# When an output block is stored, and which bank one head's product uses: attention and a gated feed-forward on one core

## The chip, the cores and the metric

The kernel runs on one core of a Trainium2 chip. The time is device microseconds for one execution. Engines are named as in the profile: PE (matrix products), PEld (its weight loads), DVE, ACT, POOL, and the queues SP, ACTq and POOLq that issue transfers. A line number such as L828 is a line of the kernel before.

## The reference

The inputs are q, k, v of shape (8, 8, 576, 64): 8 batches, 8 heads, 576 positions, 64 features. The attention is causal by blocks of 64 positions; its output is laid out as 4608 tokens of 512 features and goes through a gated feed-forward. All in float32:

```python
scores = scale * np.matmul(q, k.transpose(0, 1, 3, 2))
scores = np.where(block_i >= block_j, scores, -1e9)      # blocks of 64
attn = softmax(scores)
x = np.matmul(attn, v).transpose(0, 2, 1, 3).reshape(4608, 512)
gate = np.maximum(x @ w_gate, 0.0)                        # 512 -> 1536
val = x @ w_val
out = (gate * val) @ w_out                                # 1536 -> 512
```

## The kernel before

**Two streams of work, one order written by hand.** The attention of batch b runs beside the feed-forward of an earlier tile. A generator, `ffn_gen`, yields after nearly every feed-forward product; a table `AT` gives each step of the attention a place counted in such yields, and the loop at the end (L1515) runs the feed-forward up to that place and then the step. So every engine's instructions stand in the order in which Python writes them.

**The attention.** A round r = 4 b + hp is one pair of heads. Its visit (`s` in the table) makes the scores: the third part goes to a bank of "one" and a bank of "ffn", the first and second to two tiles of "sc". ACT makes exponentials of the third and the first at once, and of the second at the step `e`. DVE or POOL zeroes corners (`c`), steps `a` and `b` multiply the two heads with v (L586, L600), in a bank that the table `HOW` names, and DVE normalises (L523, L525, L532). A transfer transposes the result into xT.

**The matrix product's banks.** There are three pools of accumulators in PSUM: "sc" has two tiles of two banks each, "one" one bank, "ffn" three banks. A tile of a pool takes a buffer that is free again; its first writer waits for the last reader of the tenant before.

**The feed-forward.** Tiles 0 to 7 are the first 512 tokens of each batch, tile 8 (j = B) is the 64 last tokens of all eight. For f from 0 to 11 it makes gate and value, four products each (L858), ACT applies relu to the gate (L868), and DVE multiplies with the value (L878, "hidden f"); both accumulators are "ffn" banks. From f = 4 on, DVE also makes sums and differences of hidden blocks (L743). Gate 10 below is the gate of f = 10.

**The output of tiles 2 to 8.** Token rows and output columns are halved, and seven products of quarter matrices replace eight (`seven_products`). Four output blocks come of it, each 128 x 512 in an "ob" buffer, of which there are four: g (upper left), c12, c22 and c21. In order: ACT copies y into g (L815), DVE adds z (L816) and subtracts m1 (L819); ACT copies y again into c12 (L822); POOL makes c22 = g + c12 (L825); ACT copies z into c21 (L828); POOL adds c21 to g (L830); DVE adds m6 to c22 (L833) and subtracts m7 from g (L838). In tile 8 the last product and subtraction are split in halves (L842, L847).

**The stores.** `store_later` keeps one store in hand: it issues the one in hand and keeps the new one. A store of tiles 2 to 7 is one transfer of 256 KB on ACT's queue (L664). A store of tile 8 is two transfers, one on ACT's queue and one on SP's (L672). The last block of a tile, g, is therefore in hand until the c12 of the next tile is copied, and that of tile 8 until the end of the program (L1521).

Of the kernel before, what the change touches and what calls it, by code (L numbers as in the profile page):

```python
# [17 lines left out]
def kernel(  # L18
# [10 lines left out]
    nc = tc.nc  # L29

    B, H, S, D = q.shape
# [8 lines left out]
    SEVEN = 2  # L40
# [600 lines left out]
    store, late = [], []  # L641
# [16 lines left out]
    def put_block(j, hi, n0, ob, p0, p1):  # L658

        n = slice(n0, n0 + 256)  # L660
        rows = ob.rearrange("q (p n) -> q p n", n=256)
        if j < B:
            r0 = S * j + 256 * hi + 128 * p0
            nc.scalar.dma_start(  # L664
                out[r0 : r0 + 128 * (p1 - p0), n].rearrange("(p q) n -> q p n", q=128),
                rows,
            )
        else:
            by_batch = out.rearrange("(b s) n -> b s n", b=B)
            for i in range(2):  # L670
                b0 = 4 * hi + 2 * p0 + i
                (nc.scalar, nc.sync)[i].dma_start(  # L672
                    by_batch[b0 : b0 + 2 * (p1 - p0) - 1 : 2, 512:576, n].rearrange(
                        "b s n -> s b n"
                    ),
                    rows[64 * i : 64 * i + 64],
                )
# [84 lines left out]
    def seven_products(j, quads, sums):  # L762

        def times(to, which, p, c, first):
            two = wo[c // 2][:, 2 * (c % 2) : 2 * (c % 2) + 2, :]
            t = sevens[c // 2][:, 768 * (c % 2) : 768 * (c % 2) + 768]
            right = {
                5: two[:, 1, 256:512],
                2: two[:, 0, 0:256],
                1: t[:, 0:256],
                3: two[:, 0, 256:512],
                4: two[:, 1, 0:256],  # L780
                6: t[:, 256:512],
                7: t[:, 512:768],
            }[which]
            nc.tensor.matmul(  # L784
                to,
                sums.of(c)[which][:, 128 * p : 128 * p + 128],
                right,
                start=first,
                stop=(c == 5),
                skip_group_check=True,  # L790
            )

        def half(to, p):
            return to[:, 256 * p : 256 * p + 256]

        def whole(to, which, new=True, cs=range(6)):
            for p in range(2):
                for c in cs:
                    times(half(to, p), which, p, c, new and (p, c) == (0, 0))
                    if c % 2:  # L800
                        yield

        def store_later(hi, n0, ob, p0=0, p1=2):
            if store:
                store.pop()()
            store.append(lambda: put_block(j, hi, n0, ob, p0, p1))

        y = psum_ffn.tile([128, 512], FP, name="ffnp")
        z = psum_one.tile([128, 512], FP, name="one")
        for to, which in ((y, 5), (z, 2)):  # L810
            yield from whole(to, which, cs=range(4))
        for to, which in ((y, 5), (z, 2)):
            yield from whole(to, which, new=False, cs=(4, 5))
        g = sb.tile([128, 512], FP, name="ob", bufs=4)
        nc.scalar.copy(g, y)  # L815
        nc.vector.tensor_tensor(out=g, in0=z, in1=g, op=AX.add)  # L816
        m1 = psum_ffn.tile([128, 512], FP, name="ffnp")
        yield from whole(m1, 1)
        nc.vector.tensor_tensor(out=g, in0=m1, in1=g, op=AX.subtract)  # L819
        yield from whole(y, 3, new=False)  # L820
        c12 = sb.tile([128, 512], FP, name="ob", bufs=4)
        nc.scalar.copy(c12, y)  # L822
        store_later(0, 256, c12)
        c22 = sb.tile([128, 512], FP, name="ob", bufs=4)
        nc.gpsimd.tensor_tensor(out=c22, in0=g, in1=c12, op=AX.add)  # L825
        yield from whole(z, 4, new=False)
        c21 = sb.tile([128, 512], FP, name="ob", bufs=4)
        nc.scalar.copy(c21, z)  # L828
        store_later(1, 0, c21)
        nc.gpsimd.tensor_tensor(out=g, in0=g, in1=c21, op=AX.add)  # L830
        m6 = psum_ffn.tile([128, 512], FP, name="ffnp")
        yield from whole(m6, 6)
        nc.vector.tensor_tensor(out=c22, in0=m6, in1=c22, op=AX.add)  # L833
        store_later(1, 256, c22)
        if j < B:
            m7 = psum_ffn.tile([128, 512], FP, name="ffnp")
            yield from whole(m7, 7)
            nc.vector.tensor_tensor(out=g, in0=g, in1=m7, op=AX.subtract)  # L838
            store_later(0, 0, g)
        else:  # L840
            for p in range(2):
                m7 = psum_ffn.tile([128, 512], FP, name="ffnp")[:, 0:256]  # L842
                for c in range(6):
                    times(m7, 7, p, c, c == 0)
                    if c % 2:
                        yield
                nc.vector.tensor_tensor(  # L847
                    out=half(g, p), in0=half(g, p), in1=m7, op=AX.subtract
                )
                store_later(0, 0, half(g, p), p, p + 1)  # L850

    def ffn_gen():
        for j in range(B + 1):
# [3 lines left out]
            def product(to, t, c, f):  # L857
                nc.tensor.matmul(  # L858
                    to,
                    (wg, wv)[t][f // 4][:, c, 128 * (f % 4) : 128 * (f % 4) + 128],  # L860
                    x[:, c],
                    start=(c == 0),
                    stop=(c == 3),
                )

            def relu(gate):
                gate_sb = sb.tile([128, 512], BF, name="gate_sb", bufs=3)
                nc.scalar.activation(gate_sb, gate, AF.Relu)  # L868
                return gate_sb
# [3 lines left out]
            def hidden(gate_sb, val):  # L873
                if len(hT) % 4 == 0:
                    quads.append(sb.tile([128, 4, 512], BF, name="hT", bufs=3))
                h = quads[-1][:, len(hT) % 4, :]
                products.append(
                    nc.vector.tensor_tensor(out=h, in0=gate_sb, in1=val, op=AX.mult)  # L878
                )
                hT.append(h)  # L880
# [52 lines left out]
            for f in range(first, 12):  # L933
                gate = (
                    psum_one.tile([128, 512], FP, name="one")
                    if (j, f) == (1, 2)
                    else psum_ffn.tile([128, 512], FP, name="ffnp")
                )
                val = psum_ffn.tile([128, 512], FP, name="ffnp")
                for t, c in [(t, c) for t in range(2) for c in range(4)]:  # L940
                    product((gate, val)[t], t, c, f)
                    if (t, c) == (0, 3):
                        gate_sb = relu(gate)
                        if sums and f >= 4:
                            sums.step(f)
                    if (t, c) == (1, 3):
                        hidden(gate_sb, val)
                    yield
# [38 lines left out]
    def outs(j):  # L987
        full = [(s, 0, 512) for s in range(4)]
        return full if j < B else full[:3] + [(3, 0, 352), (3, 352, 512)]

    gen = ffn_gen()

    def ffn(n):
        for _ in range(n):
            if next(gen, 0) == 0:
                return
# [11 lines left out]
    dve, act, pool = nc.vector.tensor_copy, nc.scalar.copy, nc.gpsimd.tensor_copy  # L1008
# [7 lines left out]
    with tc.manual_schedule(engines={E.PE, E.DVE, E.Activation, E.Pool, E.SP}):  # L1016
# [82 lines left out]
        def mains_1(hp):  # L1099
# [259 lines left out]
            "r10": ("dve", "one", "ffn", None),  # L1359
            "r11": ("dve", "one", "ffn", None),  # L1360
            "r12": ("dve", "ffn", "sc", None),
            "r13": ("dve", "sc", "ffn", None),
            "r14": ("dve", "ffn", "ffn", None),
            "r15": ("pool", "sc", "sc", None),
            "cv21/1": "dve",
# [152 lines left out]
            place[0] = max(place[0], at)  # L1518
            acts[n]()
        ffn(10**6)  # L1520
        store.pop()()  # L1521
# [1 line left out]
_INS = ['q', 'k', 'v', 'moe_w_gate', 'moe_w_val', 'moe_w_out']  # L1523
_OUTS = [((4608, 512), 'float32')]
# [25 lines left out]
```

## Time and profile before

| | |
|---|---|
| median of 3 runs | 359.91 us (359.58 to 361.34) |
| the profiled execution's own time | 359.73 us |
| its span, first to last instruction | 357.9 us |
| granted PE clock, mean | 0.997 |
| PE, DVE, ACT, POOL busy | 342.8, 207.5, 180.1, 141.2 us |
| tile 2: products of f = 11 end, products with w_out begin | 132.2 us |
| last tile: products with w_out | 342.6 to 351.8 us |
| last tile: the two halves of g on DVE | 353.51 to 354.26 us |

The span runs from the first to the last instruction on the core; the execution's own time has about 1.8 us more around it. Busy time is the sum of an engine's instructions. The list of waits names, for an engine and line, the work whose end released it, with the total, the number of times and the longest. The chain is followed back from the last instruction: at each step to what released it. In the timeline a line is a run of like instructions: start, time, engine, line, what it writes and reads, and in brackets the idle time before it with its releaser.

### The profile page before, as it was taken

How to read it: one execution, taken by the hardware profiler on the slowest of the kernel's cores; microseconds unless marked ns; L12 is line 12 of the kernel's file. 1: busy time of each engine (PE TensorE's matmuls, PEld its weight loads, DVE VectorE, ACT ScalarE, POOL GpSimd, SP SyncE). 2: the span in 40 equal slices, each digit the busy share in tenths (PEclk: the TensorE clock that was granted, in tenths of full speed). 3: DMA queues.
4: the chain of work that ended last, by engine and by line, in shares of the span. 5: the costliest groups of instructions: out<-in, count | busy, mean ns of one | idle time of the engine just before them, and what ended most of it. 6: DMA issues, size and time to landing. Idle time of an engine off the chain costs nothing.

```text
span 357.9 us, 8015 instructions
## 1 busy us (share of the span) xinstructions
PE 342.8 (96%) x3131; PEld 202.0 (56%) x3173; DVE 207.5 (58%) x522; ACT 180.1 (50%) x286; POOL 141.2 (39%) x183
## 2 busy tenths in 40 slices
PE   6899999999999989999999999999999999999993
PEld 2544455545544558555955585557655774484472
DVE  4663445678456584467557663777266735635651
ACT  5932766686345841666256635554555523313320
POOL 4647646597848602590159103930200020020002
PEclk9999999999999999999999999999999999999998
DMA  8999999999999994899369934997400040011005
GB/s 247 296 355 373 320 222 286 194 134 174 173 226 98 148 132 125 95 145 162 82 113 146 159 76 122 135 155 97 139 16 16 16 141 0 2 60 59 1 6 143
DMA packets 155494, 50.02 MB, mean 140 GB/s; under 512 B 134464, under 2 KB 151872, under 8 KB 155456
## 3 DMA queue, kind: packets, MB, share of 16 engines
q0 software_dynamic: 70480, 8.85, 47.7%
q1 hardware_dynamic: 76432, 31.47, 42.8%
q10 hardware_dynamic: 8544, 9.18, 8.0%
q8 instruction: 25, 0.41, 0.5%
q14 instruction: 13, 0.11, 0.1%
HBM read 37.75 MB, written 9.44 MB: 132 GB/s over the span
## 4 chain that ended last, share of the span: by engine, by line
PE 87%; DMA 5%; ACT 3%; POOL 1%; DVE 1%; issue 1%; POOLq 0%; SPq 0%; DVEq 0%; ACTq 0%
PE ffnp L858 49%; PE ffnp L784 12%; PE ffnp L951 5%; PE one L784 5%; PE sc L451 3%; PE one L451 2%; PE ffnp L586 2%; DMA stage<-in_moe_w_gate_dram 2%; PE one L586 1%; DMA stage<-in_k_dram 1%; PE one L858 1%; PE sc L586 1%; PE ffnp L548 1%; ACT attnT L456 1%; DMA out_dram<-ob 1%
## 5 line engine op out<-in xcount | busy, mean ns | idle before, releaser
L878 DVE TENSOR_TENSOR hT<-gate_sb,ffnp 128x512 bf16<-128x512 bf16 x106 | 72.6, 685 | 70.0 <-PE ffnp L858 43.3
L858 PE MATMUL ffnp<-xT,wv 128*128 128x512 bf16 x357 | 99.5, 379 | 1.5 <-issue 0.6
L868 ACT ACTIVATE gate_sb<-ffnp 128x512 bf16<-128x512 f32 x103 | 62.3, 606 | 75.1 <-PE ffnp L858 75.1
L858 PE MATMUL ffnp<-xT,wg 128*128 128x512 bf16 x347 | 96.6, 379 | 1.4 <-DVE xT L630 0.3
L858 PEld LDWEIGHTS <-wv 128*128 128x128 bf16 x432 | 40.0, 98 | 45.1 <-issue 2.9
L825 POOL TENSOR_TENSOR ob<-ob 128x512 f32<-128x512 f32 x7 | 8.8, 1262 | 142.7 <-ACT ob L822 142.7
L858 PEld LDWEIGHTS <-wg 128*128 128x128 bf16 x432 | 39.8, 98 | 43.0 <-issue 3.3
L456 ACT ACTIVATE attnT<-sc 128x1024 bf16<-128x1024 f32 x56 | 57.4, 1042 | 0.0
L784 PEld LDWEIGHTS <-stage 128*128 128x128 bf16 x420 | 40.4, 98 | 6.0
L743 DVE TENSOR_TENSOR stage<-hT 128x512 bf16<-128x512 bf16 (+2 forms) x84 | 38.5, 485 | 0.9
L586 PEld LDWEIGHTS <-attnT 128*128 128x128 bf16 x640 | 26.5, 98 | 12.7 <-DVE attnT L1011 1.6
L784 PE MATMUL ffnp<-stage 128*128 128x256 bf16 x252 | 31.4, 273 | 0.0
L463 ACT ACTIVATE attnT<-one 128x512 bf16<-128x512 f32 (+1 forms) x28 | 15.0, 536 | 23.4 <-PE ffnp L451 23.3
L339 POOL DMA_DIRECT2D v_bf<-in_v_dram x30 | 24.2, 880 | 2.8 <-PE ffnp L858 1.8
L339 POOL DMA_DIRECT2D q_bf<-in_q_dram x20 | 18.2, 924 | 18.1 <-DVE hT L878 13.9
L951 PE MATMUL ffnp<-wo,hT 128*128 128x512 bf16 x90 | 22.8, 379 | 0.3
L451 PEld LDWEIGHTS <-kTm 64*128 64x128 bf16 x384 | 13.1, 94 | 15.6 <-issue 7.9
L451 PE MATMUL sc<-qTm,kTm 64*128 64x512 bf16 (+1 forms) x168 | 17.9, 305 | 1.0 <-DVE xtail L532 1.0
L339 POOL DMA_DIRECT2D k_bf<-in_k_dram x20 | 17.7, 933 | 0.0
L784 PEld LDWEIGHTS <-hT 128*128 128x128 bf16 x168 | 16.4, 98 | 1.9
L833 DVE TENSOR_TENSOR ob<-ffnp,ob 128x512 f32<-128x512 f32 x7 | 4.8, 692 | 21.6 <-POOL ob L825 15.0
L822 ACT COPY ob<-ffnp 128x512 f32<-128x512 f32 x7 | 4.1, 585 | 21.9 <-PE ffnp L784 21.9
(143 smaller groups left out, 459.4 us busy)
## 6 DMA issues: line engine op xcount, KB each, us to landing
out_dram<-ob ACTq DMA_DIRECT2D x32, 256.0 KB, 2.5
stage<-in_moe_w_val_dram SPq DMA_DIRECT2D x6, 512.0 KB, 8.2
stage<-in_moe_w_gate_dram SPq DMA_DIRECT2D x6, 512.0 KB, 8.6
stage<-in_moe_w_out_dram SPq DMA_DIRECT2D x6, 512.0 KB, 10.6
q_bf<-in_q_dram POOLq DMA_DIRECT2D x20, 128.0 KB, 4.5
k_bf<-in_k_dram POOLq DMA_DIRECT2D x20, 128.0 KB, 5.4
v_bf<-in_v_dram POOLq DMA_DIRECT2D x20, 128.0 KB, 6.5
stage<-in_v_dram SPq DMA_DIRECT2D x19, 128.0 KB, 5.6
```

The source lines that it names most:

```text
L339: ins = nc.gpsimd.dma_start(dst, part_of)
L451: nc.tensor.matmul(o, kTm[b % 2][head_of(hh), c, hp, :], qT, start=True, stop=True)
L456: return lambda: nc.scalar.activation(at[:, :, lo : lo + 512], sc, AF.Exp, scale=scale)
L463: nc.scalar.activation(at[:, hh, 1024 : 1024 + w], third[hh][:, 0:w], AF.Exp, scale=scale)
L586: nc.tensor.matmul(av[:, p, :], at[:, col : col + 128], v_bf[b % 2][:, c, h, :], start=(p == 0), stop=(c == p), skip_group_check=True,)
L743: nc.vector.tensor_tensor(out=out.rearrange("p (c n) -> p c n", c=m), in0=a, in1=b, op=op)
L784: nc.tensor.matmul(to, sums.of(c)[which][:, 128 * p : 128 * p + 128], right, start=first, stop=(c == 5), skip_group_check=True,)
L825: nc.gpsimd.tensor_tensor(out=c22, in0=g, in1=c12, op=AX.add)
L858: nc.tensor.matmul(to, (wg, wv)[t][f // 4][:, c, 128 * (f % 4) : 128 * (f % 4) + 128], x[:, c], start=(c == 0), stop=(c == 3),)
L868: nc.scalar.activation(gate_sb, gate, AF.Relu)
L878: nc.vector.tensor_tensor(out=h, in0=gate_sb, in1=val, op=AX.mult)
L951: nc.tensor.matmul(op, hT[f][:, 128 * s : 128 * (s + 1)], wo[f // 4][:, f % 4, n0:n1], start=(f == 0), stop=(f == 11),)
```

## The change

Three things. In tiles 3 to 8 the store in hand is issued behind the relu of the second gate (f = 1), so the block g of the tile before leaves there and not behind the next c12. In tile 8 nothing is kept in hand: each block's two transfers are issued where the block is made, those of c12 both on SP's queue, those of c21 both on ACT's, those of c22 and of the halves of g one on each. And the first head of round 13 (batch 3, the second pair) accumulates its product with v in an "ffn" bank instead of an "sc" tile.

```diff
@@ put_block, tile 8
-                (nc.scalar, nc.sync)[i].dma_start(
+                eng = {(0, 256): nc.sync, (1, 0): nc.scalar}.get((hi, n0))
+                (eng or (nc.scalar, nc.sync)[i]).dma_start(
@@ store_later in seven_products
             if store:
                 store.pop()()
-            store.append(lambda: put_block(j, hi, n0, ob, p0, p1))
+            if j < B:
+                store.append(lambda: put_block(j, hi, n0, ob, p0, p1))
+            else:
+                put_block(j, hi, n0, ob, p0, p1)
@@ ffn_gen, behind relu(gate)
                         if sums and f >= 4:
                             sums.step(f)
+                        if j > SEVEN and f == 1:
+                            store.pop()()
@@ HOW: corners, first head, second head, transpose
-            "r13": ("dve", "sc", "ffn", None),
+            "r13": ("dve", "ffn", "ffn", None),
@@ the end of the program
         ffn(10**6)
-        store.pop()()
+        assert not store
```

## The prediction

> **What bounds the kernel now.** I read the page first: which engine fills the span.
>
> ```profile
> span 357.9 us, 8015 instructions
> ...
> PE 342.8 (96%) x3131; PEld 202.0 (56%) x3173; DVE 207.5 (58%) x522; ACT 180.1 (50%) x286; POOL 141.2 (39%) x183
> ...
> PE 87%; DMA 5%; ACT 3%; POOL 1%; DVE 1%; issue 1%; POOLq 0%; SPq 0%; DVEq 0%; ACTq 0%
> ```
>
> PE is busy for all but 15 us, so only what makes PE wait, or what lies before its start and behind its last product, can move the time. The list of waits shows where the changed lines wait (total, times, longest, in us):
>
> ```profile
> ACT ob L828 <- DMA out_dram<-ob: 12.2, 6, 3.0
> ```
>
> The third output copy of a tile (L828, block c21) waits for a store in six of seven tiles, about 2 us each. Whether that matters differs by place. The stretches 160 to 320 show PE idle for only 0.43, 0.37, 0.53 and 0.10 us, and PE's own list of waits names none there. In the inner tiles the wait is hidden under products. At the end nothing hides it; the chain of its last microseconds:
>
> ```profile
> 347.95 0.02 ACT ob L822
> 347.96 3.44 DMA out_dram<-ob
> 351.42 0.04 ACTq L828
> 351.46 0.04 issue
> 351.50 0.59 ACT ob L828
> 352.09 0.03 POOLq L830
> 352.12 0.07 issue
> 352.19 1.30 POOLq L1545
> 353.49 0.02 issue
> 353.51 0.42 DVE ob L847
> ```
>
> Copy c21 stands behind the store of the tile before (3.44 us), and POOL's sum and DVE's subtractions behind the copy. The timeline gives what else is ready:
>
> ```profile
> 347.70 1.47 PE L784 MATMUL one<-wo,hT 128*128 128x256 bf16 x12
> ...
> 349.01 2.78 PE L784 MATMUL ffnp<-stage 128*128 128x256 bf16 x24
> 350.58 0.69 DVE L833 TENSOR_TENSOR ob<-ffnp,ob 128x512 f32<-128x512 f32 x1 [3.29 <-PE ffnp L784]
> ...
> 351.52 3.85 ACTq L672 DMA_DIRECT2D out_dram<-ob  x5
> ```
>
> Last, tile 2, for the bank edit: one visit's scores stand behind a13's normalisation.
>
> ```profile
> 127.40 0.39 PE L451 MATMUL sc<-qTm,kTm 64*128 64x384 bf16 x4 [0.99 <-DVE xtail L532]
> ...
> 128.15 0.60 ACT L868 ACTIVATE gate_sb<-ffnp 128x512 bf16<-128x512 f32 x1
> ...
> 129.08 0.69 DVE L878 TENSOR_TENSOR hT<-gate_sb,ffnp 128x512 bf16<-128x512 bf16 x1 [1.14 <-PE ffnp L858]
> ...
> 129.82 0.46 PE L586 MATMUL ffnp<-v_bf,attnT 128*128 128x65 bf16 x10
> ```
>
> **The change part by part.** All sums are against the profiled execution: 359.73 us, span 357.9, 1.8 around it; it lies 0.18 under the median 359.91.
>
> *The end of the last tile.* With tile 7's block g stored long before, an ob buffer is free and c21 waits only for its products: they end at 347.70 + 1.47 = 349.17; the c12 copy started 0.09 behind its own, so c21 runs 349.26 to 349.84 (0.585). POOL's c22 sum (1.26 from 348.61) frees POOL at 349.87, so its g sum starts 0.13 behind c21 (before: 352.09 to 352.22) at 349.98 and ends at 351.24. DVE's c22 (350.58 + 0.69) ends at 351.27. Its first half of g needs that, POOL, and six of the twelve m7 products, done at about 351.23: it runs 351.28 to 351.70. The second half needs PE's last product (351.79) and runs 351.89 to 352.30. Before it ended at 353.51 + 0.75 = 354.26: 1.96 earlier.
> The stores: each issue holds its queue (L672: ACT median 0.73, SP 0.60, the 64 KB ones 0.50 to 0.80). Before, ACT issued five from 351.52, the last starting at 354.57. After, c12's two go to SP at 348.56, c21's two to ACT: 349.88 to 351.35; c22's 0.74 to 352.10; g's first half 0.52, from 352.13; the last starts at 352.68. SP's last can start at about 352.5. So 354.57 - 352.68 = 1.89 is gained, the queue giving up 0.07 of the data's 1.96. Ten stores go before and after, and the same barriers follow. Bounds: a landing takes 2.1 to 3.1 in the L672 rows, and 2.4 for the last, so -2.2 to -1.2. I take -1.89, as like stores stand at the end of both.
> The Trainium skill, page "DMA: Bandwidth & Descriptors", section "Issuing engines are not separate DMA queues", says that stores from several engines share the same DMA engines, so a second queue saves only issue time, usually small beside the transfer. It speaks against the re-routing of c12 and c21; the rows here (0.73 of issue to 2.7 of landing) make issue a quarter. By that rule only the data's 1.96 would count, and the total would be 358.40 for 358.47.
>
> *The store at the second gate.* Six stores (g of tiles 2 to 7, 256 KB, L664) leave the place behind the c12 copy and go on ACT's queue behind the second relu of the next tile. Their data: DVE ended tile 3's g at 181.20, and tile 4's second relu starts at 184.16, so nothing waits for DVE; at the last tile it is 323.04 against 324.53. The issue (0.38, at most 0.46) runs while the relu (0.66) does, as it did beside the copy (318.06 and 318.08). Queued behind it is the third relu, which waits for PE anyway: 0.37 idle in tiles 3 to 6, 1.13 in the last two. Cost 0, covered by those waits; bounds 0 and 6 x 0.46 = 2.8 if the cover is gone. On the DMA engines it meets POOL's loads of the next q (from 184.15, landing median 4.5, so in by about 192); SP transposes them at 197.40, so 5 us of slack cover a 2.5 us store: 0. What it leaves: in tiles 3 to 7 c21 comes about 1.2 earlier (tile 3: its products end at 175.75 + 1.47, the copy started at 178.50) and DVE's g 0.7 earlier (m7 ends at 177.06 + 2.78, L838 started at 180.51). PE's idle from 160 to 320 (1.4 in all) bounds a gain; since PE names no wait there, I take 0. Tile 2's own wait (140.99) stays, as tile 1's last store is not moved.
>
> *The bank of a13* (round 13's first head). The "ffn" pool has three banks; I take it that a tenant gets the free one that the program released first. Worked through by hand, this order gives the waits that the trace shows: a14 (129.82) starts as tile 2's hidden 10 ends (129.08 + 0.69), b14 (131.31) as a14's normalisation ends (131.24). With a13 in ffn, every tenant until b14 takes a bank released later. (a) a13 takes value 8's bank, free since 123.83: 0. (b) Gate 10 (before at 125.04) takes gate 9's, whose relu runs 125.08 to 125.71: start 125.77. (c) Visit 15's third takes value 9's, whose product runs on DVE 125.97 to 126.65: start 126.71 instead of 125.79. Its other scores are free of a13, so the visit takes the 0.76 of visit 14 (121.88 to 122.64), and gate 10's last product comes at 127.47 instead of 127.72: 0.25 gained of the 0.99. (d) But ACT's exponentials follow the visit's start: first at 127.14 instead of 126.22, 0.92 later, and relu 10 stands behind three of them: it ends at 129.67 instead of 128.75. (e) Hidden 10, before at 129.08 behind PE, now waits for that relu: 129.72 to 130.40. (f) a14 takes value 10's bank: 130.46 instead of 129.82. So PE is 0.63 late from there, b14 likewise (131.94), and nothing downstream has slack. Bounds: -0.99 (the whole stall goes), and +0.92 (all of ACT's delay reaches PE). I take +0.63, from the rows that each bank waits for.
>
> Sum: 359.73 - 1.89 + 0 + 0.63 = 358.47.
>
> **The rivals.** (1) The bank edit costs nothing or gains: the 0.99 stall is the only PE wait of its kind in the list, and if banks were given in another order, (b) to (f) fall. For it: the wait is real. Against: two waits of the trace fit my order. 359.73 - 1.89 - 0 to 0.99 = 357.84 to 356.85.
> (2) Slower: the store at the second gate becomes ACT's bound. In tile 4 that relu starts 0.7 us behind its products (183.04 + 0.38 against 184.16), because exponentials stand before it, so ACT is short there. Price: the issue, 0.46 (largest L664) to 0.80 (largest L672), six times: 2.8 to 4.8, so 358.47 + that, 361.2 to 363.3. It makes the change a loss from 1.26 / 6 = 0.21 a tile on. Against: the 0.37 of idle behind the relu, and DMA issues that run beside ACT's work.
> (3) The end does not move: c21 is early, but the stores, all of the last megabyte, land no sooner. 359.73 + 0.63 = 360.36. For it: the DMA rate in the last burst is near 300 GB/s. Against: 0.5 MB are left after 351.3, under 2 us of that rate.
>
> **How the numbers follow.** A measurement of this kernel tells about 0.5% (1.8 us) from no change. Chances: the forecast 0.46, (1) 0.36, (2) 0.12, (3) 0.06. The forecast's own range is -2.2 + 0.35 to -1.2 + 0.92, 357.9 to 359.45 (0.35: half of step (d) absorbed). The range reaches from (1)'s low end to the top of the forecast's plus 0.4, by which runs of one kernel differ (359.58 to 359.91), leaving out (2) and (3) with 0.18: 356.8 to 359.9. Faster (under 358.1): nearly all of (1) and a sixth of the forecast, 0.42. Slower (over 361.7): most of (2), 0.10. The rest 0.48.
>
> **What would show it.** Right: no wait of L828 for a store in tiles 3 to 8 (one left, of 1.8, in tile 2); in the last tile c21 starting 1.3 behind c12 (now 3.55), and DVE ending 0.5 behind PE's last product (now 2.5); around gate 10 and visit 15 two PE waits (for ACT's relu, for DVE's hT) instead of one for L532, and a14 still behind hT; the third relu of each tile still waiting for PE. Wrong: tile 2's products starting at or before 132.20 (rival 1), gaps at each tile's third gate (rival 2), or the last store landing 5 us behind PE's last product, as now, instead of 3.3 (rival 3).

## The result and the profile after

The changed kernel takes 358.96 us (median of 20 runs, 358.44 to 360.43), the kernel before 359.96 us in 20 runs beside them (359.15 to 362.26). The ratio is 0.9971, 95% interval 0.9957 to 0.9985: about 1.0 us faster, where 1.26 was forecast (359.73 to 358.47).

The page of the changed kernel, lines that answer to those shown of before:

```profile
span 358.6 us, 8020 instructions
...
PE 82%; DMA 8%; ACT 5%; DVE 2%; issue 1%; POOL 0%; DVEq 0%; POOLq 0%
```

This one execution is longer than the profiled one of before (360.43 us against 359.73) although its median is shorter. The two differ ahead of any changed code: round 13's first head (a13) starts at 126.38, in before at 124.59. The transposes into xT between 84 and 106 us show where that comes from in this pair; before:

```profile
DMA to landing us min/median/max: 5.9/7.9/8.3
```

and after:

```profile
DMA to landing us min/median/max: 7.4/9.2/9.8
```

In after PE waits for two of them (1.3 us), in before for none. Over the thirteen profiles of this study a13's start lies anywhere from 124.3 to 126.8, with and without the change. So spans of single executions can't be compared here; stages that begin behind that place can. I cut each trace at two marks on PE: a13's first product to tile 2's first product with w_out (the bank edit); from there to tile 8's first such product (six tiles, the store at the second gate); and from there to the end of the span. The ratio beside them comes from repeated runs.

| kernel | bank stage | six tiles | end | ratio to before (95%) | median us |
|---|---|---|---|---|---|
| before | 7.61 | 210.26 | 15.44 | 1 | 359.96 |
| after | 8.16 | 210.23 | 13.83 | 0.9971 (0.9957 to 0.9985) | 358.96 |
| e1_no_bank | 7.60 | 210.24 | 13.81 | 0.9941 (0.9913 to 0.9970) | 358.56 |
| e2_bank_alone | 8.15 | 210.29 | 15.1 | 1.0015 (0.9993 to 1.0036) | 360.73 |
| e3_gate_alone | 7.61 | 210.22 | 13.82 | 0.9954 (0.9929 to 0.9979) | 358.55 |
| e4_last_alone | 7.61 | 210.23 | 16.02 | 0.9998 (0.9977 to 1.0020) | 360.37 |
| e5_five_bufs | 7.61 | 210.23 | 13.94 | 0.9936 (0.9913 to 0.9959) | 358.01 |
| e6_four_issues | 8.16 | 210.24 | 13.69 | 0.9990 (0.9964 to 1.0017) | 359.43 |
| e7_later_visit | 6.75 | 210.22 | 13.89 | 0.9939 (0.9912 to 0.9967) | 357.65 |
| e8_later_merged | 6.74 | 210.23 | 14.21 | 0.9936 (0.9909 to 0.9962) | 357.87 |
| e9_relu_first | 7.17 | 210.24 | 14.08 | 0.9959 (0.9939 to 0.9980) | 358.06 |
| e10_relu_first_sc | 7.39 | 210.25 | 13.87 | 0.9961 (0.9942 to 0.9980) | 358.39 |
| e11_bufs_later | 6.75 | 210.22 | 13.81 | 0.9947 (0.9925 to 0.9968) | 357.65 |

Medians of different groups of runs lie beside their own runs of before (medians 359.96, 360.52 for e1 to e4, 360.08 for e5 to e8, 359.7 for e9 and e10, 359.9 for e11), so across groups it is the ratio that compares. Ratios are good to about 0.25% (0.9 us). The first two stages repeat to a few hundredths of a us, the end to about 0.3 (before 15.44, e2 with the same end 15.1); the end also uses the span as the page gives it, to a tenth, so its hundredths are good to 0.05 only.

After against before by stages: +0.55, -0.03, -1.61, together -1.09; the ratio says -1.04.

The end, timeline of after:

```profile
350.26 0.59 ACT L826 COPY ob<-ffnp 128x512 f32<-128x512 f32 x1 [2.47 <-PE ffnp L785]
...
351.32 2.78 PE L785 MATMUL ffnp<-stage 128*128 128x256 bf16 x24
351.52 0.58 ACT L832 COPY ob<-one 128x512 f32<-128x512 f32 x1 [0.68 <-PE one L785]
352.14 3.65 ACTq L673 DMA_DIRECT2D out_dram<-ob  x5
...
354.14 0.42 DVE L851 TENSOR_TENSOR ob<-ob,ffnp 128x256 f32<-128x256 f32 x1 [0.15 <-PE ffnp L785]
```

Copy c21 (L832) now starts 1.26 us behind c12 (L826) and waits for its products; DVE's last subtraction follows PE's last product (351.32 + 2.78 = 354.10) instead of POOL. The list of waits has one wait of that copy for a store left, tile 2's:

```profile
ACT ob L832 <- DMA out_dram<-ob: 1.9, 1, 1.9
```

Accordingly the chain of the last microseconds holds PE's products nearly alone, where before it held a store, ACT, POOL and DVE:

```profile
351.49 2.63 PE ffnp L785 x24
...
354.14 0.42 DVE ob L851
```

Tile 2, timeline of after (times lie 1.79 later than in before's profile, by a13's start):

```profile
127.56 0.81 PE L862 MATMUL ffnp<-xT,wg 128*128 128x512 bf16 x2 [0.56 <-ACT gate_sb L872]
...
128.50 0.27 PE L451 MATMUL ffnp<-qTm,kTm 64*128 64x256 bf16 x1
...
128.89 0.60 ACT L463 ACTIVATE attnT<-one 128x512 bf16<-128x512 f32 x1 [1.39 <-PE ffnp L451]
...
130.77 0.62 ACT L872 ACTIVATE gate_sb<-ffnp 128x512 bf16<-128x512 f32 x1
...
131.42 0.69 DVE L882 TENSOR_TENSOR hT<-gate_sb,ffnp 128x512 bf16<-128x512 bf16 x1 [1.69 <-ACT gate_sb L872]
131.44 0.59 PE L862 MATMUL ffnp<-xT,wg 128*128 128x512 bf16 x2 [0.48 <-ACT gate_sb L872]
...
132.16 0.46 PE L586 MATMUL ffnp<-v_bf,attnT 128*128 128x65 bf16 x10
```

The one wait for L532 is gone, and in its place gate 10 waits for relu 9 (0.56), the visit's third waits for hidden 9 (which ran from 127.76 to 128.44), and relu 10, behind three exponentials, holds hidden 10 (1.69) and so a14.

### The profile page after: what moved, and what is told of

It is laid out like the page before. It is cut to its first block, busy times and chain, and to the rows that moved or that the text cites. A ratio compares the mean times of both kernels' runs of the same rounds, so it can differ in the third digit from the quotient of the medians.

```text
span 358.6 us, 8020 instructions
## 1 busy us (share of the span) xinstructions
PE 343.7 (96%) x3131; PEld 202.1 (56%) x3173; DVE 208.4 (58%) x522; ACT 180.1 (50%) x286; POOL 141.2 (39%) x183
## 4 chain that ended last, share of the span: by engine, by line
PE 82%; DMA 8%; ACT 5%; DVE 2%; issue 1%; POOL 0%; DVEq 0%; POOLq 0%
PE ffnp L862 47%; PE ffnp L785 13%; PE one L785 5%; DMA xT<-xnat 5%; PE sc L451 3%; PE one L451 2%; PE ffnp L957 2%; DMA stage<-in_moe_w_gate_dram 2%; ACT attnT L456 2%; PE ffnp L586 2%; PE one L862 1%; PE one L586 1%; PE one L1008 1%; ACT attnT L415 1%; PE sc L586 1%
## 5 line engine op out<-in xcount | busy, mean ns | idle before, releaser
L826 ACT COPY ob<-ffnp 128x512 f32<-128x512 f32 x7 | 4.1, 586 | 21.9 <-PE ffnp L785 21.9
```

## The experiments

**The theory** was that of the prediction: the end gains because a buffer is free for c21, the second gate's store costs nothing, and the bank edit loses because later tenants of the pool take banks that come free later. The rivals: the bank edit gains, the store loads ACT, or the last stores land no sooner.

**Without the bank edit (e1).** Of after, this is put back:

```diff
-            "r13": ("dve", "ffn", "ffn", None),
+            "r13": ("dve", "sc", "ffn", None),
```

> The changed kernel with the first head of round 13 back in an sc tile; both store edits stay. Theory A (the bank edit costs 0.55 us, the stores gain 1.65): from the first product of a13 to the first product of tile 2 with w_out 7.6 us as in the kernel before (8.16 in the changed one), PE waiting once, 1.0 us, for L532; the last-tile stretch (first product with w_out of tile 8 to the end of the span) 13.8 us as in the changed kernel (15.5 before); ratio to before about 0.9955. Rival B (the bank edit is free or a gain, the stores gain only what the changed kernel shows, 1.0): ratio 0.997 or above. Rival C (the gain of the stores needs the later place of the products): ratio near 1.

Measured: bank stage 7.60, end 13.81, ratio 0.9941. PE's list has the old wait again:

```profile
PE sc L451 <- DVE xtail L532: 1.0, 1, 1.0
```

The 0.99 us stall costs less than the edit that takes it away: the stage is 0.56 shorter with it.

**The bank edit alone (e2).** The same line, changed in before.

> The kernel before with only the bank of round 13's first head changed. Theory A: 8.16 us from a13 to the products of tile 2, two waits of PE for relu, a14 behind hidden 10, about 0.55 us slower (ratio 1.0015), and nothing downstream takes it back. Rival B: the L532 stall of 0.99 us goes and nothing takes its place, ratio 0.9975 to 1.000.

Measured: bank stage 8.15, ratio 1.0015; the ratio's interval contains 1 but the stage is 0.54 longer, with after's waits in PE's list:

```profile
PE ffnp L858 <- ACT gate_sb L868: 1.0, 2, 0.6
```

e1 and e2 give the same cost, with and without the other parts: a loss of 0.55 that doesn't depend on them. A gain from this edit in this order (rival 1) is out.

**The store at the second gate alone (e3).** Before, with two lines:

```diff
                             sums.step(f)
+                        if j > SEVEN and f == 1:
+                            store.pop()()
```

> The kernel before with only the store of g moved to the second gate; tile 8 keeps one store in hand as before. Theory A (c21's wait for the store of g is what holds the end; queues and immediate issue add little): c21 starts 1.3 us behind c12 in tile 8, the last-tile stretch 13.7 to 14.0 us, ratio about 0.9955. Rival D (the end is held by the issues on ACT's queue, so that the immediate issue on two queues is needed): stretch 14.5 or more, ratio 0.998. Rival E (the store at the second gate holds ACT): gaps of PE of 0.2 or more a tile behind the third gate, tile 3 to 6 over 37.4 us each.

Measured: six tiles 210.22, end 13.82, ratio 0.9954. Copy c21 starts 1.26 behind c12 (349.57 and 350.83), as in after. The whole gain of the end comes from this part. The re-routed and immediate stores of the last tile add nothing measurable (13.82 here, 13.83 in after). The Trainium skill, page "DMA: Bandwidth & Descriptors", section "Issuing engines are not separate DMA queues", says that issuing from several engines saves only the time to issue. These two runs agree with it, but they test little of it: both use two queues with five issues on each, and differ only in which block goes to which.

**The last tile's part alone (e4).** Before, with the routing, the immediate stores of the last tile and its new ending; tile 7's last store stays behind c12:

```diff
-                (nc.scalar, nc.sync)[i].dma_start(
+                eng = {(0, 256): nc.sync, (1, 0): nc.scalar}.get((hi, n0))
+                (eng or (nc.scalar, nc.sync)[i]).dma_start(
...
-            store.append(lambda: put_block(j, hi, n0, ob, p0, p1))
+            if j < B:
+                store.append(lambda: put_block(j, hi, n0, ob, p0, p1))
+            else:
+                put_block(j, hi, n0, ob, p0, p1)
```

> The kernel before with only tile 8 changed: every store issued where its block is made, c12 on SP's queue, c21 on ACT's. The store of tile 7's g still leaves behind c12 of tile 8. Theory A: c21 still waits 3 us for that store, so the end stays within 0.3 us of before (stretch 15.2 to 15.6), ratio 0.999 to 1.000. Rival D (the queues hold the end): stretch 14.5 or less, ratio 0.997.

Measured: end 16.02, against 15.44 of before; ratio 0.9998. ACT's queue and ACT at the end:

```profile
350.18 0.38 ACTq L664 DMA_DIRECT2D out_dram<-ob  x1
...
354.05 0.59 ACT L832 COPY ob<-one 128x512 f32<-128x512 f32 x1 [3.30 <-PE ffnp L785]
```

c21 waits for tile 7's store, issued 3.87 before it (the trace names PE, but those products had ended at 349.92 + 1.47 = 351.39, and the store landed at 353.95); POOL and DVE follow it, DVE's last two subtractions from 356.06. So this part without the other one doesn't help; it ends 0.6 later than before. About half of that is the store's landing, 3.77 behind its issue where before had 3.44 and e2, with the same program there as before, 3.08: this landing is also what parts the ends of before and e2. The rest is in ACT's queue: its five issues behind c21 now follow each other without a gap, and the last begins 0.34 later behind c21's start than in before.

**A fifth buffer, and every store where it was (e5).** Before, with five buffers in the five places that allocate ob:

```diff
-        c21 = sb.tile([128, 512], FP, name="ob", bufs=4)
+        c21 = sb.tile([128, 512], FP, name="ob", bufs=5)
```

> The kernel before with five output buffers instead of four; every store stays where it was. Theory A (c21 waits for a free buffer and for nothing else): c21 starts 1.3 us behind c12 in tile 8 though the store of tile 7's g still leaves just behind c12; stretch from tile 8's products to the end 13.7 to 14.1 us (before 15.4), ratio about 0.9955. Rival F (the store of g itself, 256 KB among the last stores, holds the end, so it had to leave earlier): c21 early, but the stretch 14.6 or more, ratio 0.998 or above.

Measured: end 13.94, ratio 0.9936, and no wait of c21 for a store:

```profile
347.84 0.59 ACT L822 COPY ob<-ffnp 128x512 f32<-128x512 f32 x1 [2.52 <-PE ffnp L784]
347.86 0.38 ACTq L664 DMA_DIRECT2D out_dram<-ob  x1
349.11 0.59 ACT L828 COPY ob<-one 128x512 f32<-128x512 f32 x1 [0.68 <-PE one L784]
```

Tile 7's store still leaves with c12, and c21 starts 1.27 behind c12 all the same. What the change bought at the end is a free buffer; when the store is issued doesn't matter in itself, to within the 0.3 that the end repeats to.

**Four issues in place of one (e6).** After, with a tile's last store cut in four:

```diff
-            nc.scalar.dma_start(
+            for h in range(0, 128, 32) if (hi, n0) == (0, 0) else (None,):
+                qs = slice(None) if h is None else slice(h, h + 32)
+                nc.scalar.dma_start(
```

> The changed kernel with the store of g at the second gate split into four transfers of 64 KB, so that ACT's queue is held there four times: about 1.4 us in place of 0.38 in each of six tiles. Theory A (up to about 1.0 us is covered by the relu before it and the wait of the third relu): the third relu about 0.4 us late in tiles 3 to 6, PE's tiles there at most 0.4 us longer each, ratio to before 0.997 to 1.002. Rival E (ACT is the bound at that place): 1.0 us more a tile in tiles 3 to 6, ratio 1.008.

Measured: six tiles 210.24, to 210.23. ACT's engine and queue around tile 4's second gate:

```profile
184.67 0.34 ACTq L666 DMA_DIRECT2D out_dram<-ob  x1
...
185.53 0.93 ACTq L666 DMA_DIRECT2D out_dram<-ob  x2
186.51 0.60 ACT L876 ACTIVATE gate_sb<-ffnp 128x512 bf16<-128x512 f32 x1 [0.54 <-PE ffnp L866]
```

The four issues (the second at 185.05) take 1.71 us of the queue up to 186.46. The third relu starts 0.05 behind the last of them and 0.21 behind its products (185.27 + 1.03), in after 0.04 behind. So here the queue does hold it, though the trace names PE: ACT is idle before it for 0.54 to 0.71 in tiles 3 to 6, in after for 0.37, which makes the relu 0.17 to 0.34 late. PE's tiles keep their 37.38 us all the same. So what covers the issue on ACT is used up by four issues, and PE still has room behind it; one issue of 0.38 is well inside both. Rival 2, which charged 0.46 to 0.80 for each of six, is out.

**The visit later (e7).** e1, with round 15's scores due 4 units later, so that they come behind gate 10 and value 10 and a13's normalisation has time:

```diff
-            "s15": 371.65,
+            "s15": 375.65,
```

> The changed kernel with round 13's first head back in sc, and the visit of round 15 four feed-forward products later (place 375.65 in place of 371.65), so that gate 10's last and value 10's first three products run while a13 is normalised, and relu 10 stands in front of the exponentials. Theory A: PE waits about 0.35 us for L532 instead of 1.0, a13 to the products of tile 2 about 7.0 us (7.6 before, 8.16 in the changed kernel); ratio to before about 0.994. Rival G (ACT, not a13's bank, sets that stretch): 7.6 us or more, as the exponentials come later; ratio 0.9955 or above.

Measured: bank stage 6.75, ratio 0.9939, median 357.65. The wait for L532 has fallen from 0.99 to 0.09, too short for PE's list, and relu 10 is in front of the exponentials:

```profile
125.85 0.60 ACT L872 ACTIVATE gate_sb<-ffnp 128x512 bf16<-128x512 f32 x1 [0.39 <-PE ffnp L862]
126.85 0.60 ACT L463 ACTIVATE attnT<-one 128x512 bf16<-128x512 f32 x1 [0.40 <-PE ffnp L451]
```

So 0.90 less of the stall made the stage 0.85 shorter than in e1; the way to have it was the order, not the bank. Against after, the stage is 1.41 shorter.

**One store less on each queue (e8).** e7, with the last block stored once, behind both subtractions:

```diff
-                store_later(0, 0, half(g, p), p, p + 1)
+            store_later(0, 0, g)
```

> The same as the later visit, and tile 8's g stored whole once both halves are subtracted (two transfers of 128 KB in place of four of 64 KB). If the last issues are held by the queues (0.6 us behind their data in the changed kernel): the last issue starts 0.5 to 0.6 us earlier, its landing takes 0.2 to 0.3 longer, and the stretch to the end is 13.4 to 13.6 us (13.8 in the changed kernel). If the landing is bound by the bytes: 13.8 or more.

Measured: end 14.21, e7 13.89. A miss: ACT's last issue starts 9.86 behind tile 8's first w_out product, in e7 10.46, so 0.60 earlier as expected, and yet the end came no sooner. The last pair of stores shows why. Its landing in e8, then in e7:

```profile
DMA to landing us min/median/max: 2.8/3.0/3.1
```

```profile
DMA to landing us min/median/max: 2.2/2.3/2.3
```

ACT's last store landed 3.13 behind its issue, in e7 2.23: the landing took back 0.90, more than the 0.60 that the issue gave and far more than the 0.2 to 0.3 expected. Whether that is the 128 KB in place of 64, or that both queues issue at once (352.54 and 352.55), was not tried: of the pair before it, also 128 KB each and also issued at once, one landed after 2.56 and one after 2.86.

**Only relu 10 moved (e9, e10).** To tell step (d) from the bank waits: the visit one unit later, first in after (a13 in ffn, e9), then in e1 (a13 in sc, e10):

```diff
-            "s15": 371.65,
+            "s15": 372.65,
```

> The changed kernel (a13 in ffn) with the visit of round 15 one feed-forward product later (place 372.65 in place of 371.65), so behind gate 10's last product: relu 10 then stands in front of the visit's exponentials on ACT. Theory A, step by step: gate 10 still waits for relu 9 and the visit for hidden 9 (both banks unchanged), but hidden 10 no longer waits for a relu behind three exponentials, so a14 comes about 1.1 us earlier; a13 to the products of tile 2 about 7.1 us (8.16 in the changed kernel). Rival H (the two bank waits in front of the visit are the whole cost): 8.1 us.

> The same one-product shift with a13 in sc, as in the kernel before. Theory A: the wait for L532 stays (the visit's second part needs a13's buffer), about 0.8 us instead of 1.0; hidden 10 was bound by PE there and not by relu 10, so little is gained behind it: a13 to the products 7.2 to 7.5 us (7.6 before). Rival H: 7.4 to 7.6, the same kernel within 0.2.

Measured: 7.17 in e9, to 8.16 in after. ACT in e9 has the relu ahead of the exponentials,

```profile
127.65 0.60 ACT L872 ACTIVATE gate_sb<-ffnp 128x512 bf16<-128x512 f32 x1 [1.11 <-PE ffnp L862]
...
128.14 0.59 ACT L463 ACTIVATE attnT<-one 128x512 bf16<-128x512 f32 x1
```

while gate 10's wait for relu 9 is in PE's list as in after:

```profile
PE ffnp L862 <- ACT gate_sb L872: 0.6, 1, 0.6
```

The visit's third still comes just behind hidden 9 (127.55 behind 126.79 + 0.68), but gate 10's last product now fills that time: value 10 starts 2.90 behind a13, in after 3.09 (129.47 - 126.38). That is 0.19 of the 0.99 by which after's stage is longer; the other 0.80 is the relu's place behind the exponentials. e10 gives 7.39, 0.21 less than e1, by a wait for L532 of 0.78 in place of 0.99. With this order a13 in ffn is the better by 0.22, where in the old order it is the worse by 0.56 (after against e1). e7's later place beats both.

**Fifth buffer and later visit (e11).** Before with the edits of e5 and e7, so that no store is moved:

> The kernel before with two edits only: five output buffers, and the visit of round 15 four products later. No store is moved. Theory A: the two gains lie in different places and add up: a13 to the products of tile 2 6.75 us, the stretch from tile 8's products to the end 13.7 to 14.1, the inner tiles unchanged (210.2), 2.4 us in all, ratio about 0.9935. Rival I (the earlier arrival of PE at the end runs into another wait): the stretch 14.5 or more.

Measured: 6.75, 210.22 and 13.81; ratio 0.9947, median 357.65. Its stages equal those of e7 to within what they repeat to. e5, e7, e8 and e11 can't be told apart by their ratios; by stages e7 and e11 are the shortest, about 2.5 below before and 1.4 below after. Against before repeated runs show it too; against after they don't, as the intervals overlap, and there it rests on the stages of one execution each.

## Why the prediction was nearly right

*The end of the last tile (-1.89; measured -1.61).* Mechanism right: c21 starts 1.26 behind c12 (1.3 said), DVE ends 0.46 behind PE's last product (0.5 said). From tile 8's first w_out product to DVE's end it is 11.80 before (354.26 - 342.46) and 9.79 after (354.56 - 344.77): -2.01, for 1.96 worked out. The mis-sized term is the queue's share. To the start of ACT's last issue it is 12.11 before (354.57) and 10.46 after (355.23 - 344.77), -1.65: the queue gave back 0.36 of the data's gain, for 0.07. The step that was off is "g's first half 0.52": that issue held the queue for 0.79. Issues of one form took 0.50 to 0.80 in the rows I had; with a queue of five behind each other, the range and not the one row was the thing to take. It was no accident of one execution either: the same issue took 0.79 to 0.86 in all nine profiles in which c21 comes early and g leaves in halves. The last store lands at 357.49, 2.26 behind its issue; before it was 2.28 (not the 2.4 that was said), so the landing added nothing. That is 3.4 behind PE's last product, where 3.3 was said and 5 would have meant rival 3, which thereby falls.

*The store at the second gate (0; measured -0.03 over six tiles, the same in e3).* Right, and for the reason given: the third relu still waits for PE by 0.37. In tiles 3 to 6 the issue is over before the second relu even starts (148.84 and 149.10), where the prediction had it beside the relu. e6 shows that the cover has room to spare for one issue. The L828 waits of tiles 3 to 7 went, and nothing came of that, as PE's silence about them had said.

*The bank (+0.63; measured +0.55).* Right step by step. Shifted by a13's 1.79, gate 10 was to start at 127.56 and did; the visit's third at 128.50, and did; relu 10 was to end at 131.46 and ended at 131.39; a14 was to start at 132.25 and started at 132.16. The 0.08 between forecast and result is in step (d): the first exponential came 0.04 early and the relu's end 0.07. One wait was not in the list: gate 11 waits 0.48 for relu 10's bank as hidden 10 does, at the same moment, so that it costs nothing of its own. e9 shows that step (d), not the banks' waits in (b) and (c), decides the sign: with the relu in front the same edit gains 0.22 (e9 against e10). The chance of 0.36 for rival 1 was high beside a working that matched two waits of the trace.

*The sum.* -1.26 said, -1.09 by stages and -1.04 by the ratio. Both misses, the queue's 0.28 and the bank's 0.08, are within the bounds given.

## What to carry to other kernels

When a wait is removed by giving a tile another buffer of a rotating pool, follow every later tenant of that pool, and then the engine whose work starts earlier or later as a result: here two short bank waits were cheap, and a relu that slid behind three exponentials turned a 0.2 us gain into a 0.55 us loss. If a copy waits for a buffer at the end of a kernel, try one more buffer first: here it did as much as moving the store (e5), and needed no reordering. Cut traces into stages between marks on the bounding engine: here the two stages ahead of the end repeated to hundredths of a us where whole executions differed by 2.5.

## What was not expected of the hardware

ACT's queue issued a transfer ahead of instructions that stand before it in the program. In after the store stands behind the second gate's relu, and in tiles 3 to 6 its issue runs before that relu starts:

```profile
148.46 0.38 ACTq L664 DMA_DIRECT2D out_dram<-ob  x1
...
149.10 0.66 ACT L872 ACTIVATE gate_sb<-ffnp 128x512 bf16<-128x512 f32 x1
```

The issue begins 0.09 behind the end of the products that this relu waits for (147.99 + 0.38), while ACT still has earlier exponentials to run. In the last two tiles ACT has no such work, and the issue begins 0.06 behind the relu's start. What stands behind the issue does wait for it: in e6 four issues, 1.71 us of queue time, made the third relu 0.17 to 0.34 late.

The up to 2.5 us by which executions differ before a13 are in part waits for transposes by DMA: in after for those into xT of tile 1, whose median landing was 9.2 us where before had 7.9, in e3 and e8 for one into kTm (1.4 and 1.0 us). What delays them was not tried and stays open.

The ten stores at the end, of two sizes, held their queues for 0.56 to 0.79 us each in after and 0.50 to 0.80 in before. The length goes with the place in the order (in before ACT's last issue is the long one, in after the last but one); what sets it was not tried either.
